# Top-k attention with two gated layers on one core: mask and exponential of the top-k moved from VectorE to two ScalarE passes

## The chip, the cores and the metric

One core of a Trainium2 chip runs the whole program. The metric is the device time of one execution in microseconds; the median of three runs is quoted. Engine names are those of the profile: PE is TensorE's matmul, PEld its weight load, DVE is VectorE, ACT is ScalarE, POOL is GpSimd, SP issues the DMAs.

## What is computed

The reference is an attention over the 32 largest scores of each row, a feed-forward layer with SiLU, and eight experts whose outputs are mixed by gates that are balanced in eight rounds. The change touches the attention alone:

```python
batch, n_heads, seq, head_dim = (2, 8, 576, 64)
scores = scale * np.matmul(q, k.transpose(0, 1, 3, 2))          # scale = 1 / 8
kth = np.partition(scores, -top_k, axis=-1)[..., -top_k:-top_k + 1]   # top_k = 32
mask = scores >= kth
scores = np.where(mask, scores, -1000000000.0)
scores = scores - np.max(scores, axis=-1, keepdims=True)
attn = np.exp(scores)
attn = attn / (np.sum(attn, axis=-1, keepdims=True) + 1e-09)
return np.matmul(attn, v).astype(np.float32)
```

The 1152 rows of attention output then go through x @ w_in, SiLU, @ w_out (512 to 2048 to 512), and each expert is relu(x @ w1[e]) @ w2[e] (512 to 1024 to 512), summed with its gate.

## The kernel before

The 1152 tokens are nine tiles of 128. Attention runs in five groups of queries, each over four pairs of heads. A unit is one group and one pair of heads; its score tiles are 128 queries by all 576 keys, 72 such tiles in all (64 of one head each, 8 half tiles that hold 64 queries of both heads of a pair). `score_tile` (L313) makes one of them:

- PE writes the scores into PSUM (L320), ACT copies them to an SBUF tile `s` (L323), of which the pool holds `SB` = 5.
- DVE finds the 32 largest by four rounds of eight: `max` (L332), and between rounds `match_replace` (L339), which overwrites the eight found in a work tile `w`.
- After the first round the largest value is known. A little row on POOL (on DVE in the first group, where `soon` is set) makes -scale * max (L335), and ACT takes the exponential of all 576 scores into a second tile `e` (L337), while DVE goes on searching.
- After the fourth round DVE compares the scores with the 32nd and multiplies by the exponentials in one instruction, which also gives the row's sum (L342).
- 1e-9 is added (L344, POOL or DVE), DVE takes the reciprocal (L345), ACT scales the row (L347), PE transposes it (L350, L352), ACT copies the transpose (L363, L364), and when a unit's tiles are done PE multiplies with V (L360, tile `pav`).

A scheduler orders the instructions of every engine ahead of time, by priorities that the kernel sets (`tc.cur_priority`), and each engine runs its list in order. Attention has the first claim; between its rows stand matmuls of the feed-forward layer and of experts as filler, in steps of a hidden block of weights: 12 matmuls of 128x256 (L145 to L149, `mm3`) into a PSUM bank, an activation on ACT and a split into two parts on ACT and POOL (L137, L138), then the second product (128x512 rows of L147 to L149), with weights that SP's queue loads. After the last unit of attention the rest of the filler runs, and from about 660 us on seven experts by a seven-product scheme.

The feed-forward weights come as 64-bit words in 32 blocks. Each is loaded into one of four buffers (`RAWB`, L529), converted by ACT (`narrow`, L493; the low word on POOL at L499 or on ACT at L497), and joined on DVE (L502). From block 12 on the joining rows are held until the last reciprocal of the first query group (`held`, L758, through `tc.issue_after`).

Of the kernel before, what the change touches and what calls it, by code (L numbers as in the profile page):

```python
# [8 lines left out]
F32 = mybir.dt.float32  # L9
# [3 lines left out]
AF = mybir.ActivationFunctionType  # L13
ALU = mybir.AluOpType
# [3 lines left out]
P = 128  # L18
TOPK = 32
# [19 lines left out]
WB = 4  # L39
RW = 6  # L40

SB = 5
SW = 2
AB = 2

# [27 lines left out]
def topk_attention_moe_sinkhorn_kernel(  # L73
# [12 lines left out]
    nc = tc.nc  # L86
    B, H, S, D = q.shape
# [6 lines left out]
    NTT = NT // P  # L94
    SH = S // 2
    SCALE = 1.0 / D ** 0.5
    MASKED = -1e9 / SCALE
    W = DM
    assert NDC * P == W

# [7 lines left out]
    const = ctx.enter_context(tc.tile_pool(name="const", bufs=1))  # L108
# [1 line left out]
    make_identity(nc, ident)  # L110
    ones = const.tile([P, P], F32, name="ones")
    nc.gpsimd.memset(ones, 1.0)
    neg = const.tile([P, 1], F32, name="neg")
    nc.gpsimd.memset(neg, MASKED)
    wg_raw = const.tile([P, NDC, NE], F32, name="wg_raw")
    wgH = const.tile([P, NDC, NE], F32R, name="wgH")
    wgL = const.tile([P, NDC, NE], F32R, name="wgL")
# [78 lines left out]
    sp = att.enter_context(tc.tile_pool(name="sp", bufs=SW))  # L196
# [116 lines left out]
    def score_tile(nm, qq, qL, kk, js, cols, soon, behind=None, late=False):  # L313

        ps = ps_s.tile([P, 2, 512], F32, name=f"ps_{nm}", tag="s")

        for j in js:
            for part, a in enumerate((qq, qL)):
                for hh in range(2):
                    nc.tensor.matmul(ps[:, hh, 0:SH], a[:, j, cols], kk[:, j, hh * SH : (hh + 1) * SH],  # L320
                                     start=j == js[0] and part == 0, stop=j == js[-1] and part == 1)
        s = sp.tile([P, S], F32, name=f"s_{nm}", tag="s", bufs=SB)
        copied.append(nc.scalar.activation(s.rearrange("p (a c) -> p a c", a=2), ps[:, :, 0:SH], AF.Copy))  # L323
        w = sp.tile([P, S], F32, name=f"w_{nm}", tag="w")
        m8 = small.tile([P, TOPK], F32, name=f"m8_{nm}", tag="m8")
        sm = small.tile([P, 4], F32, name=f"sm_{nm}", tag="sm")
        e = sp.tile([P, S], F32, name=f"e_{nm}", tag="e")
        src = s
        tiny = nc.vector if soon else nc.gpsimd
        for r in range(TOPK // 8):  # L330
            mr = m8[:, 8 * r : 8 * r + 8]
            nc.vector.max(mr, src)  # L332
            if r == 0:

                tiny.tensor_scalar(sm[:, 0:1], m8[:, 0:1], -SCALE, None, op0=ALU.mult)  # L335
                with tc.issue_after(behind.ins) if behind and late else nullcontext():
                    nc.scalar.activation(e, s, AF.Exp, scale=SCALE, bias=sm[:, 0:1])  # L337
            if r < TOPK // 8 - 1:
                nc.vector.match_replace(out=w, in_to_replace=mr, in_values=src, imm_value=-3e38)  # L339
                src = w  # L340

        nc.vector.scalar_tensor_tensor(s, s, m8[:, TOPK - 1 : TOPK], e, op0=ALU.is_ge, op1=ALU.mult,  # L342
                                       accum_out=sm[:, 1:2])
        tiny.tensor_scalar(sm[:, 2:3], sm[:, 1:2], 1e-9, None, op0=ALU.add)  # L344
        normal.append(nc.vector.reciprocal(sm[:, 3:4], sm[:, 2:3]))  # L345
        with tc.issue_after(behind.ins) if behind else nullcontext():
            nc.scalar.activation(s, s, AF.Copy, scale=sm[:, 3:4])  # L347
        pt = ps_t.tile([P, 4, P], F32, name=f"pt_{nm}", tag="tr")
        for c in range(4):
            nc.tensor.transpose(pt[:, c, :], s[:, c * P : (c + 1) * P], ident)  # L350
        pt2 = ps_t.tile([P, P], F32, name=f"pt2_{nm}", tag="tr")
        heads.append(nc.tensor.transpose(pt2, s[:, S - P : S], ident))  # L352
        return pt, pt2
# [793 lines left out]
```

## Time and profile before

| | |
|---|---|
| runs | 1222.16, 1222.31, 1222.91 us; median 1222.31 |
| profiled execution | 1223.83 us, of which the span from the first to the last instruction is 1222.0 |
| PE busy | 1176.0 us (96%), weight loads 949.6 |
| DVE, ACT, POOL busy | 800.5 (66%), 609.2 (50%), 593.2 (49%) |
| granted TensorE clock | 0.992 of full speed over the span |

Busy times are those of the profiler: a PE row is listed until its modelled end and overlaps the next, and rows of ACT and DVE overlap their neighbours by some hundredths to a tenth of a microsecond. The page also cuts the span into 40 slices of 30.6 us and gives each engine's busy share in tenths. DVE is at 9 from slice 2 to slice 16, with one exception at the first, and falls to 2 and 0 there: that is attention. PE is at 9 or more from slice 4 to the end.

```
PE   5797999999999999999999999999999999999998
DVE  7989999999999999203567634634445345344444
ACT  6856887788876877643313332332323223323212
```

### The profile page before, as it was taken

The numbers are of one execution on the slowest core, as the hardware profiler recorded it, in microseconds if no ns is written. First come the engines' busy times: TensorE is split into PE (matmuls) and PEld (weight loads), VectorE is DVE, ScalarE is ACT, GpSimd is POOL, SyncE is SP. The second block draws the span as 40 slices with busy tenths as digits, with TensorE's granted clock in tenths as the row PEclk, the third lists the DMA queues.
The fourth block names the chain that finished last, engine by engine and source line by source line (L and its number), as shares of the span: only waits on it lengthen the run. The fifth ranks groups of instructions, "written<-read, shape, count | busy, mean of one in ns | idle before, by whom it ended". The sixth has DMA issues, their size and how long they took to land.

```text
span 1222.0 us, 17930 instructions
## 1 busy us (share of the span) xinstructions
PE 1176.0 (96%) x6122; PEld 949.6 (78%) x6122; DVE 800.5 (66%) x1543; ACT 609.2 (50%) x1241; POOL 593.2 (49%) x665
## 2 busy tenths in 40 slices
PE   5797999999999999999999999999999999999998
PEld 3664666788778888888787888888888888888887
DVE  7989999999999999203567634634445345344444
ACT  6856887788876877643313332332323223323212
POOL 6666766788634843530546444445334444353310
PEclk9997999999999999999999999999999999999999
DMA  9889777998786898899814221121111211211001
GB/s 268 292 285 323 261 245 235 323 333 288 232 304 236 274 323 293 288 325 375 293 56 129 76 80 35 52 72 49 52 52 37 84 35 35 70 52 53 18 1 69
DMA packets 131723, 210.91 MB, mean 173 GB/s; under 512 B 23472, under 2 KB 69552, under 8 KB 131632
## 3 DMA queue, kind: packets, MB, share of 16 engines
q1 hardware_dynamic: 131632, 209.77, 51.4%
q8 instruction: 48, 0.79, 0.3%
q14 instruction: 43, 0.35, 0.1%
HBM read 170.15 MB, written 39.58 MB: 172 GB/s over the span
## 4 chain that ended last, share of the span: by engine, by line
PE 82%; DVE 11%; ACT 2%; DMA 1%; POOL 1%; issue 1%; SPq 0%; POOLq 0%; ACTq 0%; DVEq 0%
PE h L147 9%; PE h L148 9%; PE h L149 9%; PE bank L147 5%; PE bank L149 5%; PE bank L148 5%; PE yA L149 4%; PE yB L149 4%; PE yB L147 4%; PE yA L147 4%; PE yA L148 4%; PE yB L148 4%; PE bank L598 4%; DVE m L332 3%; PE pav L360 3%; DVE w L339 3%
## 5 line engine op out<-in xcount | busy, mean ns | idle before, releaser
L138 POOL TENSOR_TENSOR wp<-rw,wp 128x512 fp32r<-128x512 f32 (+1 forms) x56 | 86.7, 1567 | 195.2 <-ACT wp L137 195.2
L332 DVE MAX8 m<-w 128x8 f32<-128x576 f32 x192 | 140.0, 745 | 0.7
L138 POOL TENSOR_TENSOR wa<-raw,wa 128x512 fp32r<-128x512 f32 x88 | 114.9, 1318 | 29.6 <-ACT wa L137 14.2
L138 POOL TENSOR_TENSOR w<-rw,w 128x512 fp32r<-128x512 f32 x56 | 72.0, 1290 | 92.0 <-ACT w L137 92.0
L339 DVE MATCH_REPLACE8 w<-m,w 128x576 f32<-128x576 f32 x128 | 94.4, 739 | 0.0
L978 DVE SCALAR_TENSOR_TENSOR gL_0b<-gB,gH_0b 128x512 fp32r<-128x512 f32 (+1 forms) x56 | 44.5, 794 | 55.7 <-ACT gH_0b L977 54.8
L147 PE MATMUL yB<-w,gH_0b 128*128 128x512 f32 x208 | 80.9, 389 | 0.0
L148 PE MATMUL yB<-w,gH_0b 128*128 128x512 f32 x208 | 80.9, 389 | 0.0
L149 PE MATMUL yB<-w,gL_0b 128*128 128x512 f32 x208 | 80.1, 389 | 0.0
L977 ACT ACTIVATE gH_0b<-gB 128x512 fp32r<-128x512 f32 (+1 forms) x56 | 33.6, 600 | 76.1 <-PE yB L148 41.4
L148 PE MATMUL h<-x1L,wp 128*128 128x512 f32 x168 | 65.6, 391 | 0.0
L149 PE MATMUL h<-x1H,wp 128*128 128x512 f32 x168 | 65.6, 390 | 0.0
L147 PE MATMUL h<-x1H,wp 128*128 128x512 f32 x168 | 65.6, 390 | 0.0
L991 DVE TENSOR_TENSOR gB<-u,h 128x512 f32<-128x512 f32 x56 | 38.5, 687 | 35.6 <-PE h L149 35.5
L342 DVE SCALAR_TENSOR_TENSOR s<-s,m,e 128x576 f32<-128x576 f32 x64 | 61.2, 956 | 0.5
L137 ACT ACTIVATE w<-rw 128x512 fp32r<-128x512 f32 x56 | 34.6, 627 | 49.8 <-PE yB L149 48.3
L147 PE MATMUL bank<-xH,wa 128*128 128x256 f32 x192 | 57.2, 298 | 1.8 <-DVE g_m L449 1.1
L598 PE MATMUL bank<-wb,gT_e 128*128 128x512 f32 x128 | 58.2, 594 | 0.0
L347 ACT ACTIVATE s<-s,sm 128x576 f32<-128x576 f32 x64 | 49.9, 781 | 15.3 <-DVE sm L345 15.0
L137 ACT ACTIVATE wa<-raw 128x512 fp32r<-128x512 f32 x88 | 55.0, 648 | 3.2 <-DMA raw<-in_moe_w_dram 2.5
L138 DVE TENSOR_TENSOR wp<-sp,wp 128x1024 fp32r<-128x1024 f32 x28 | 45.3, 1617 | 15.3 <-ACT wp L137 15.3
L337 ACT ACTIVATE e<-s,sm 128x576 f32<-128x576 f32 x64 | 50.1, 784 | 8.4 <-DVE s L342 4.5
(376 smaller groups left out, 3670.6 us busy)
## 6 DMA issues: line engine op xcount, KB each, us to landing
wa<-sk SPq DMA_DIRECT2D x64, 512.0 KB, 5.5
wb<-sk SPq DMA_DIRECT2D x64, 512.0 KB, 5.3
rw<-in_moe_w_dram SPq DMA_DIRECT2D x112, 256.0 KB, 2.7
raw<-in_moe_w_dram SPq DMA_DIRECT2D x80, 256.0 KB, 3.8
wb<-in_moe_w_dram SPq DMA_DIRECT2D x32, 512.0 KB, 5.1
sk<-wa SPq DMA_DIRECT2D x24, 512.0 KB, 3.9
sk<-wb SPq DMA_DIRECT2D x24, 512.0 KB, 4.2
wfr<-in_moe_w_in_dram SPq DMA_DIRECT2D x16, 512.0 KB, 6.0
```

The costliest lines, as they stand in the source:

```text
L137: nc.scalar.activation(dH, src, AF.Copy)
L138: eng.tensor_sub(dL, src, dH.bitcast(F32))
L147: nc.tensor.matmul(ps, wH, xH, start=first, stop=False, skip_group_check=more)
L148: nc.tensor.matmul(ps, wH, xL, start=False, stop=False, skip_group_check=more)
L149: return nc.tensor.matmul(ps, wL, xH, start=False, stop=last, skip_group_check=more)
L332: nc.vector.max(mr, src)
L337: nc.scalar.activation(e, s, AF.Exp, scale=SCALE, bias=sm[:, 0:1])
L339: nc.vector.match_replace(out=w, in_to_replace=mr, in_values=src, imm_value=-3e38)
L342: nc.vector.scalar_tensor_tensor(s, s, m8[:, TOPK - 1 : TOPK], e, op0=ALU.is_ge, op1=ALU.mult, accum_out=sm[:, 1:2])
L347: nc.scalar.activation(s, s, AF.Copy, scale=sm[:, 3:4])
L598: nc.tensor.matmul(y, gT[:, c * P : (c + 1) * P], b[c], start=F == 0 and c == 0, stop=F == nF - 1 and c == NDC - 1)
L978: nc.vector.scalar_tensor_tensor(gL, src, 0.0, gH.bitcast(F32), op0=ALU.max, op1=ALU.subtract)
```

## The change

The exponential no longer runs beside the search. After the fourth round a little row makes scale * (32nd - max) from the 32nd value and the largest. ACT then takes two passes over `s` in place. The first is a parametric rectifier of 32nd - score: a score below the 32nd gives a positive difference, which is kept, and a score at or above it a difference of zero or less, which is multiplied by 2^-80. The second is an exponential with a scale of -scale * 2^80: it brings the kept scores' differences back to their size, and turns every other difference into an argument so far below zero that the result is zero. The second pass gives the row's sum. The compare-and-multiply on DVE, the tile `e` and its two buffers are gone; the tiles `s` go from 5 to 7. An unused constant goes as well.

```diff
-SB = 5
+SB = 7
-    MASKED = -1e9 / SCALE
+    BELOW = 2.0**-80
-    neg = const.tile([P, 1], F32, name="neg")
-    nc.gpsimd.memset(neg, MASKED)
...
-        e = sp.tile([P, S], F32, name=f"e_{nm}", tag="e")
         src = s
         tiny = nc.vector if soon else nc.gpsimd
         for r in range(TOPK // 8):
             mr = m8[:, 8 * r : 8 * r + 8]
             nc.vector.max(mr, src)
-            if r == 0:
-
-                tiny.tensor_scalar(sm[:, 0:1], m8[:, 0:1], -SCALE, None, op0=ALU.mult)
-                with tc.issue_after(behind.ins) if behind and late else nullcontext():
-                    nc.scalar.activation(e, s, AF.Exp, scale=SCALE, bias=sm[:, 0:1])
             if r < TOPK // 8 - 1:
                 nc.vector.match_replace(out=w, in_to_replace=mr, in_values=src, imm_value=-3e38)
                 src = w
-
-        nc.vector.scalar_tensor_tensor(s, s, m8[:, TOPK - 1 : TOPK], e, op0=ALU.is_ge, op1=ALU.mult,
-                                       accum_out=sm[:, 1:2])
+        kth = m8[:, TOPK - 1 : TOPK]
+        tiny.tensor_scalar(sm[:, 0:1], kth, m8[:, 0:1], SCALE, op0=ALU.subtract, op1=ALU.mult)
+
+        with tc.issue_after(behind.ins) if behind and late else nullcontext():
+            nc.scalar.activation(s, s, AF.Prelu, scale=-1.0, bias=kth, alpha=BELOW)
+            nc.scalar.activation(s, s, AF.Exp, scale=-SCALE / BELOW, bias=sm[:, 0:1], accum_out=sm[:, 1:2])
         tiny.tensor_scalar(sm[:, 2:3], sm[:, 1:2], 1e-9, None, op0=ALU.add)
```

The scheduler makes a new order of it. Two places follow. Names are tile<-tiles read, the last number of a name is the tile's instance and differs between the two programs; `wf_24` is weight block 24 in both, `s_0_0_3_1` the score tile of group 0, pair 3, second head. Lines after the change are two to five lower.

ACT at the end of the first query group, before: the exponentials of the last two tiles (`e_0_0_3_...`) stand ahead of block 24, the last of them in the first row here, and only their scaling by the reciprocal (L347, the last two rows) behind it.

```order
L337 ACTIVATE e_0_0_3_1_0_591<-s_0_0_3_1_0_586,sm_0_0_3_1_0_590 128x576
L347 ACTIVATE s_0_0_2_0_0_460<-s_0_0_2_0_0_460,sm_0_0_2_0_0_464 128x576
L493 ACTIVATE wf_23_639<-wfr_23_797 128x512
L347 ACTIVATE s_0_0_2_1_0_493<-s_0_0_2_1_0_493,sm_0_0_2_1_0_497 128x576
L493 ACTIVATE wf_24_638<-wfr_24_803 128x512
L363 ACTIVATE aT_0_0_2_0_453<-pt_0_0_2_0_0_479 128x4x128
L364 ACTIVATE aT_0_0_2_0_453<-pt2_0_0_2_0_0_484 128x128
L323 ACTIVATE s_1_0_0_0_1_1665<-ps_1_0_0_0_1_1660 128x576
L363 ACTIVATE aT_0_0_2_1_454<-pt_0_0_2_1_0_517 128x4x128
```

The same place now: L337 is the rectifier, L338 the exponential with the sum, L342 the scaling, L488 the conversion.

```order
L337 ACTIVATE s_0_0_3_0_0_545<-s_0_0_3_0_0_545,m8_0_0_3_0_0_548 128x576
L488 ACTIVATE wf_23_629<-wfr_23_787 128x512
L342 ACTIVATE s_0_0_2_1_0_486<-s_0_0_2_1_0_486,sm_0_0_2_1_0_490 128x576
L337 ACTIVATE s_0_0_3_1_0_577<-s_0_0_3_1_0_577,m8_0_0_3_1_0_580 128x576
L488 ACTIVATE wf_24_628<-wfr_24_793 128x512
L358 ACTIVATE aT_0_0_2_0_447<-pt_0_0_2_0_0_472 128x4x128
L338 ACTIVATE s_0_0_3_0_0_545,sm_0_0_3_0_0_549<-s_0_0_3_0_0_545,sm_0_0_3_0_0_549 128x576
L359 ACTIVATE aT_0_0_2_0_447<-pt2_0_0_2_0_0_477 128x128
L321 ACTIVATE s_1_0_0_1_1_1718<-ps_1_0_0_1_1_1713 128x576
L338 ACTIVATE s_0_0_3_1_0_577,sm_0_0_3_1_0_581<-s_0_0_3_1_0_577,sm_0_0_3_1_0_581 128x576
```

Both rectifiers now stand ahead of block 24, and both exponentials with the sum behind it.

PE just ahead of the last product with V (`pav_4_1_3`), before: the filler beside it belongs to the feed-forward layer of group 3, its weight tile `wa` number 412.

```order
L147 MATMUL bank2_134<-xH_3_5098,wa_412_5888 128x256
L148 MATMUL bank2_134<-xL_3_5099,wa_412_5888 128x256
L149 MATMUL bank2_134<-xH_3_5098,wa_412_5888 128x256
L360 MATMUL pav_4_1_3_6874<-aT_4_1_3_0_6740,vn_1_3_3732 64x256
L360 MATMUL pav_4_1_3_6874<-aT_4_1_3_1_6741,vn_1_3_3732 64x256
```

The same place now: the filler beside it is still the second product of an expert, `wb` number 393.

```order
L145 MATMUL bank1_131<-wb_393_4925,gH_e0_3_4_4940 128x512
L146 MATMUL bank1_131<-wb_393_4925,gH_e0_3_4_4940 128x512
L147 MATMUL bank0_130<-wb_393_4925,gL_e0_3_4_4941 128x512
L147 MATMUL bank1_131<-wb_393_4925,gL_e0_3_4_4941 128x512
L355 MATMUL pav_4_1_3_6800<-aT_4_1_3_0_6670,vn_1_3_3695 64x256
L355 MATMUL pav_4_1_3_6800<-aT_4_1_3_1_6671,vn_1_3_3695 64x256
```

Ahead of that product stand 46 matmuls of 512 columns and 92 of 256 fewer than before; all other rows there are as many. They follow after it.

## Rows read from the trace of the kernel before

**Rows 1.** The page, busy times, share of the span, number of instructions.
```profile
PE 1176.0 (96%) x6122; PEld 949.6 (78%) x6122; DVE 800.5 (66%) x1543; ACT 609.2 (50%) x1241; POOL 593.2 (49%) x665
```

**Rows 2.** Chain of waits, three PE pieces: start us, us on the chain, what.
```profile
215.06 0.23 PE bank L147
...
249.28 0.12 PE bank L147
...
504.90 1.88 PE pav L360 x16
```

**Rows 3.** Windows: stretch, length, busy us of each engine, clock, DMA share, GB/s.
```profile
core 0: us, PE busy (x) PEld busy (x) DVE busy (x) ACT busy (x) POOL busy (x), PEclk, DMA share, GB/s
120.00:500.00 380.00, 374.91 (x2341) 293.00 (x2340) 370.38 (x826) 302.00 (x664) 234.01 (x316) 1.00 0.82 279
500.00:660.00 160.00, 155.73 (x876) 130.56 (x875) 61.49 (x132) 60.62 (x139) 65.88 (x67) 0.99 0.71 248
660.00:1222.00 562.00, 558.03 (x2463) 461.75 (x2461) 261.96 (x353) 164.35 (x281) 218.48 (x203) 1.00 0.18 53
```

**Rows 4.** Groups by line, whole run: busy us, mean ns | idle before.
```profile
L342 DVE SCALAR_TENSOR_TENSOR s<-s,m,e 128x576 f32<-128x576 f32 x64 | 61.2, 956 | 0.5
L342 DVE DVE_READ_ACCUMULATOR s<-s,m,e 128x1 f32 x64 | 5.0, 78 | 0.0
L337 ACT ACTIVATE e<-s,sm 128x576 f32<-128x576 f32 x64 | 50.1, 784 | 8.4 <-DVE s L342 4.5 <-POOL sm L335 3.6
L447 ACT ACTIVATE t_m<-bank 128x256 f32<-128x256 f32 x48 | 18.6, 388 | 26.1 <-PE bank L149 25.7
L452 ACT ACTIVATE t_m<-t_m 128x256 f32<-128x256 f32 x32 | 13.7, 428 | 0.0
L364 ACT ACTIVATE aT<-pt_h 128x64 f32<-128x64 f32 x16 | 2.9, 248 | 0.0
```

**Rows 5.** Windows of one line alone: L342 on DVE twice, L337 on ACT.
```profile
0.00:68.00 68.00, 7.33 (x16) 0.97 0.91 291
...
120.00:500.00 380.00, 61.20 (x120) 1.00 0.82 279
...
120.00:500.00 380.00, 45.61 (x58) 1.00 0.82 279
```

**Rows 6.** Timeline of ACT near the first group's end: start us, us, instruction [idle before].
```profile
59.04 0.67 ACT L493 ACTIVATE wf<-wfr 128x512 f32<-128x512 f32 x1 [0.57 <-DMA wfr<-in_moe_w_out_dram]
59.62 0.76 ACT L337 ACTIVATE e<-s,sm 128x576 f32<-128x576 f32 x1
60.29 0.76 ACT L347 ACTIVATE s<-s,sm 128x576 f32<-128x576 f32 x1
...
63.55 0.67 ACT L493 ACTIVATE wf<-wfr 128x512 f32<-128x512 f32 x1 [1.16 <-DMA wfr<-in_moe_w_out_dram]
64.12 0.57 ACT L363 ACTIVATE aT<-pt 128x512 f32<-128x512 f32 x1
64.60 0.26 ACT L364 ACTIVATE aT<-pt 128x128 f32<-128x128 f32 x1
64.76 0.65 ACT L323 ACTIVATE s<-ps 128x576 f32<-128x576 f32 x1
```

**Rows 7.** Windows of 40 us, columns as in rows 3.
```profile
400.00:440.00 40.00, 37.34 (x251) 31.94 (x250) 39.20 (x87) 35.60 (x82) 32.01 (x42) 1.00 0.86 292
...
560.00:600.00 40.00, 39.28 (x249) 33.17 (x247) 14.79 (x29) 13.82 (x31) 10.03 (x10) 1.00 0.94 347
```

**Rows 8.** Waits in 120 to 500 us: who for whom, us, times, longest.
```profile
ACT t_m L447 <- PE bank L149: 13.2, 15, 2.9
...
ACT e L337 <- POOL sm L335: 3.6, 5, 1.7
...
POOL sm L344 <- DVE s L342: 24.5, 12, 4.7
```

**Rows 9.** Chain of waits, end of the first group.
```profile
67.83 3.61 DVE wf L502 x6
```

**Rows 10.** Timeline of ACT, first instruction.
```profile
0.71 1.28 ACT L250 ACT_TABLE_LOAD   x1 [0.71 <-PEq L1131]
```

## The prediction

> **What bounds the kernel now.** I read the page first, then the windows by stage, then the chain of waits, and only then single lines. The page [rows 1] shows TensorE (PE) busy 96% of the span, which is not the bound it seems: the listed ends of matmuls are modelled and overlap, while on the chain of waits a 512-column one counts 0.23 us and a 256-column one 0.12 [rows 2], so a busy PE may still stand still between two rows. The windows [rows 3] tell the stages apart. From 120 to 500 us (attention of query groups 1 to 4, with feed-forward filler in between) VectorE (DVE) is the engine that is never free: 370.4 of 380 us, 97.5%, where ScalarE (ACT) has 302.0, 79%. The first query group ends on DVE as well: the chain of waits goes from its last rows there into the conversion of the weights [rows 9]. From 500 us on DVE has little to do, and after 660 us PE has 558.0 of 562: that last part can't be touched by this change. Attention is therefore the only place to win, and DVE the engine that sets its pace.
>
> **The change, part by part.**
>
> *DVE.* The compare-and-multiply goes, 72 times (64 and 8 of the half tiles; the 64 average 956 ns [rows 4]), with its accumulator read. By stage it is 61.2 us in 120 to 500 and 7.33 us in the first group [rows 5]. DVE in 120 to 500 falls to 370.4 - 61.2 = 309 us, 81% of the old length: it stops being the bound.
>
> *ACT.* One exponential becomes a rectifier and an exponential with a sum: one more pass over 128x576 for each of the 58 tiles of that stretch [rows 5]. A pass is listed with 0.78 us [rows 4], but its successor starts 0.67 us after it (59.62 to 60.29 [rows 6]); I take 58 x 0.67 = 38.9 us. The read of ACT's accumulator is nowhere in this trace. Its bounds are zero and the smallest copy of ACT, 0.25 us (128x64 [rows 4]); I take 0.1, of the order of DVE's own read, 78 ns [rows 4]: 58 x 0.1 = 5.8 us.
>
> *Order.* The scheduler puts attention earlier. Counted in the two orders, 46 matmuls of 512 columns and 92 of 256 fewer stand ahead of the last probability-times-V product on PE: 46 x 0.23 + 92 x 0.12 = 21.6 us of PE work that must be done later, at the pace of 500 to 660 us (155.7 of 160 us busy [rows 3]), so 22.2 us. Twelve of the 256-column ones make a step, so 7.7 steps move, with their ACT work (a tanh of 0.39 us and up to three copies of 0.43 [rows 4], 12.9 us in all) and their loads, two of 512 KB a step on SP's queue, 8.1 MB: at the 347 GB/s of 560 to 600 us [rows 7] that is 23.2 us beside PE's 22.2, so SP's queue is no worse a limit than PE by more than 1 us.
>
> *ACT's new sum* in the stretch: 302.0 + 38.9 + 5.8 - 12.9 = 333.8 us. It becomes the fullest engine, and the stretch lasts 333.8 us divided by the share that it can be kept busy. Below is the fullest 40 us that ACT has now, 35.6 of 40, 89%, with DVE at 98% beside it [rows 7]; above is what DVE reached as the bound, 97.5%. I take 95%, nearer the upper one, because ACT now mostly waits for PE (13.2 us for the tanh alone [rows 8]): it has caught up with its supplier, and an engine with a backlog does not wait so. 333.8 / 0.95 = 351.4 us, 28.6 less than 380.
>
> *The first group.* DVE loses 7.33 us of work here, and I count almost nothing of it. The conversion of the feed-forward weights waits for the last reciprocal of this group and starts at 67.83 us [rows 9]. In the new order the last two exponentials stand on ACT behind the conversion of weight block 24, and that row waits for its DMA: now it starts at 63.55 us after 1.16 us of idling for the transfer [rows 6]. Behind it, by the spacings in [rows 6]: its own 0.57, a copy 0.48, exponential 0.77, small copy 0.16, copy 0.65, exponential 0.77, then about 0.35 for addition and reciprocal on DVE: 67.3 us. Gain 0.5 us. If block 24 came as much earlier as DVE is faster, the gain would be 7.33 less the two ACT passes of the last tile (about 1.5) and their handing over, some 5 us; that is the other bound. The block follows a ring of four buffers, not the top-k, so I stay at 0.5.
>
> *Small edits at nothing.* The negated maximum becomes a subtract-and-multiply of the same 128x1 size on the same engine. The two buffers of the exponential go and the scores get seven instead of five: a tile now keeps its scores through two more ACT passes, some 2 us, with a new tile every 380 / 58 = 6.6 us, and the two added buffers cover it; without them ACT's copy of the next scores would wait.
>
> *Sum.* -28.6 + 22.2 - 0.5 = -6.9 us, against the profiled execution's 1223.83 us, which lies 1.5 us above the median of the runs (1222.31): 1216.9 there, **1215.4 us** as a median.
>
> *A rule against the change.* The 64 compare-and-multiplies average 956 ns on DVE, and an ACT pass of the same 128x576 averages 784 [rows 4]: by the rows, work of 61.2 us leaves DVE and 44.7 comes to ACT. The Trainium skill, in "ScalarE: Activation LUTs" under the rules for kernel authors, says that rectifiers, maxima and products belong on VectorE, which it puts at up to about three times faster per element in bf16. By that rule ACT would be given what DVE does in a third of its pass, 58 x 0.26 = 15 us, and the trade would be 15 off for 44.7 on; these float32 rows show no such lead of DVE.
>
> **The rivals.**
>
> *A, the forecast.* ACT is kept busy 94 to 97.5% of the stretch, which then lasts 355.1 to 342.4 us: 1219 to 1206 us.
>
> *B, the first group gains too.* Weight block 24 comes earlier with everything else, and some 5 us come off instead of 0.5: 1211 us. For it: transfers of the later blocks wait for buffers that conversions free. Against it: the DMA wait in [rows 6] at a moment when DVE was the late one.
>
> *C, a draw.* At 93.2% the stretch is 358.3 us, 21.7 shorter, and the matmuls that were moved behind it take all of that back: 1222 us. What shrinks is then only the wait, and it reappears as filler. For it: ACT and PE hand single PSUM buffers to each other, so neither can run far ahead.
>
> *D, slower: ACT's queue stops at the exponential.* In the old order the exponential needed the maximum of the first round and had the whole search to hide POOL's little subtraction. Now the subtraction starts after the 32nd value is known, on POOL's queue behind splits, and the exponential waits for it in ACT's queue, with evacuations of PE's banks behind it. ACT has waited 3.6 us, 5 times, for such a POOL row already, and POOL 24.5 us for DVE's sum [rows 8], which becomes a wait for ACT. If each of the 58 exponentials costs ACT 0.25 us of waiting, 14.5 us, the stretch is 365.9, and the sum -14.1 + 22.2 - 0.5: 7.6 us slower, 1230 us. Above 0.16 us a tile (9.3 us) it decides for slower. The orders put several rows between rectifier and exponential, which speaks against it.
>
> *E, the function tables.* If the rectifier needed another table than the exponential, each tile would load two. The one load of this trace took 1.28 us [rows 10], so 144 loads are 184 us: 1406 us. Against it: rectifier and exponential already follow each other at 59.04 and 59.62 us with no load in between [rows 6], and both orders hold a single load. The Trainium skill says the same price in "ScalarE: Activation LUTs", What ACT_TABLE_LOAD costs: about 1.28 us and a drain of about 1.38 for a switch to a different set, which would make it 383 us here; the trace agrees on the first and has no switch to show the second.
>
> **How the numbers follow.** A measurement of this kernel tells a change from none at about 0.2%, 2.4 us. Faster by more needs ACT above 93.8%, slower by more below 92.5%. I give A 0.47 (0.02 of it within 2.4 us), B 0.10, C 0.15, D 0.27, E 0.01. So faster 0.45 + 0.10 = 0.55; same 0.02 + 0.15 = 0.17; slower 0.28. With ACT at 97.5% and a free accumulator read the stretch is 328.0 / 0.975 = 336.4, the time 1200; with 89% and a read of 0.25 us it is 342.5 / 0.89 = 384.8, the time 1249. Of these ends I leave 1 in 10 on either side: 1203 to 1232; the forecast's own range is 1206 to 1219.
>
> **What would show it.** Right: in 120 us to the end of attention DVE's share falls to about 88% and ACT's rises to 95%; the last probability-times-V product, now at 504.9 us [rows 2], comes near 476; rows of PE after it are the filler that was moved, 22 us longer; the weight conversion still starts at about 67 us. Wrong: ACT below 92% with idle time before the exponential put down to POOL (D), or the conversion starting at 62 us (B); a second table load (E). The whole falls if the stretch is not shorter at all, that is, if DVE never set its pace, or if PE stalls behind 500 us where the moved work goes.

## The result, and the profile after

The changed kernel took 1239.24 us (median of 4 runs, 1238.70 to 1240.08) where the kernel before took 1222.24 beside it: 1.0139 times as long, 95% interval 1.0122 to 1.0157. It is slower by 17 us; the forecast was 1215.4, range 1203 to 1232. The profiled execution took 1239.21 us with a span of 1237.4, 15.4 more than before.

First the busy times of the page, as in [rows 1]: DVE did lose 58 us and ACT gained 46, and PE is as full as it was.

```profile
PE 1186.5 (96%) x6122; PEld 950.0 (77%) x6122; DVE 742.9 (60%) x1399; ACT 655.4 (53%) x1385; POOL 578.3 (47%) x664
```

The windows by stage, columns as in [rows 3]:

```profile
120.00:500.00 380.00, 372.93 (x2276) 284.12 (x2276) 321.51 (x703) 338.09 (x775) 220.65 (x314) 1.00 0.79 265
500.00:660.00 160.00, 157.03 (x896) 133.08 (x895) 54.21 (x115) 60.49 (x144) 65.06 (x71) 0.99 0.74 274
660.00:1237.00 577.00, 573.11 (x2507) 469.90 (x2505) 266.63 (x367) 168.34 (x288) 225.04 (x207) 1.00 0.18 54
```

In the attention stretch ACT is now fuller than DVE, as forecast. But PE has 2276 rows there instead of 2341: it does *less* of its work in the same 380 us. What PE gets done there turns out to matter, not DVE's share. The engine shares of the chain of waits point the same way; before:

```profile
PE 82%; DVE 11%; ACT 2%; DMA 1%; POOL 1%; issue 1%; SPq 0%; POOLq 0%; ACTq 0%; DVEq 0%
```

and after:

```profile
PE 88%; DVE 5%; ACT 3%; DMA 3%; issue 1%; POOL 0%; SPq 0%; ACTq 0%; POOLq 0%
```

These shares take in the expert phase, where PE is nearly alone. In 120 to 500 us by itself the chain ran over PE for 76% and over DVE for 15% before, and runs over them for 89% and 6% now: over PE for the most part even when DVE was listed at 97.5%. Only in the first 120 us was DVE the larger part (61% before).

**An account by PE.** Both kernels give PE the same 6122 matmuls. I valued each kind (source line and shape) at the spacing that it usually has in the kernel before (the 30th percentile of start to next start: 227 ns for most rows of 512 columns, 119 for 256, 132 for 288, 108 to 112 for most transposes). The sum is 1119.7 us for either kernel. What is left of a stage's length is PE's stall (waits, and rows that ran at the lower of TensorE's two clocks, 1.2 instead of 2.4 GHz). Stages are bounded by the first probability-times-V row of the 5th unit (group 1's first), the last such row, and the first ACT copy of expert 0.

| stage | before: length = rows + stall | after | difference |
|---|---|---|---|
| to the 5th unit | 127.2 = 67.4 + 59.8 | 133.6 = 72.3 + 61.3 | +6.4 |
| 5th to last unit | 381.0 = 352.7 + 28.2 | 363.0 = 326.3 + 36.6 | -18.0 |
| to expert 0 | 138.4 = 129.0 + 9.4 | 160.6 = 150.5 + 10.1 | +22.2 |
| experts, end | 575.4 = 570.6 + 4.9 | 580.2 = 570.6 + 9.7 | +4.8 |
| sum | 1222.0 = 1119.7 + 102.4 | 1237.4 = 1119.7 + 117.7 | +15.4 |

So the attention stretch is 18 us shorter because 26.4 us of PE's rows left it (4.9 went ahead of it, 21.5 behind), and it is worse inside by 8.4 us of stalls. The rest is 4.8 us in the expert phase, where the change touches nothing, 1.5 in the first part and 0.7 in the third.

**Where PE waits.** The longest wait in the stretch is at 330 us. ACT's timeline there (start us, us, instruction):

```profile
328.24 0.68 ACT L358 ACTIVATE aT<-pt 128x512 f32<-128x512 f32 x1
328.72 1.76 ACT L135 ACTIVATE wa<-raw 128x512 fp32r<-128x512 f32 x3
330.28 0.86 ACT L337 ACTIVATE s<-s,m 128x576 f32<-128x576 f32 x1
330.94 0.85 ACT L342 ACTIVATE s<-s,sm 128x576 f32<-128x576 f32 x1
331.61 0.36 ACT L359 ACTIVATE aT<-pt 128x128 f32<-128x128 f32 x1
331.76 0.86 ACT L338 ACTIVATE s<-s,sm 128x576 f32<-128x576 f32 x1
332.43 0.29 ACT L338 ACTIVATION_READ_ACCUMULATOR s<-s,sm 128x1 f32 x1
332.52 0.73 ACT L321 ACTIVATE s<-ps 128x576 f32<-128x576 f32 x1
```

and PE's, those rows that waited:

```profile
332.02 0.33 PE L347 MATMUL pt<-ident,s 128*128 128x128 f32 x1 [2.14 <-ACT aT L359]
333.31 0.85 PE L318 MATMUL ps<-kk,qq 128*128 128x288 f32 x2 [0.96 <-ACT s L321]
```

ACT has no idle time here. The copy that empties the transpose bank (L359) stands behind three weight splits, a rectifier and a scaling, and PE's next transpose waits 2.14 us for it; the score matmuls wait another 0.96 for L321, behind an exponential. At these two waits the granted clock fell; the window, columns as in [rows 3]:

```profile
330.00:340.00 10.00, 7.02 (x20) 4.12 (x21) 9.69 (x22) 8.92 (x19) 4.25 (x7) 0.83 0.47 148
```

A clock of 0.83 over 10 us is 3.4 us at the lower level, 1.2 GHz, which adds up to 1.7 us to the stall; in the kernel before the whole stretch ran at 2.4 GHz [rows 3]. So a wait of PE can cost more than its own length. This one place is shown; how the rest of the 8.4 us is spread was not worked out row by row.

ACT's own waits, 120 to 500 us:

```profile
ACT t_m L442 <- PE bank L147: 8.2, 10, 1.3
...
ACT s L338 <- POOL sm L334: 0.6, 1, 0.6
```

and POOL's:

```profile
POOL sm L339 <- ACT s L338: 40.1, 26, 3.3
```

ACT waited once, 0.6 us, for POOL's subtraction; POOL's small addition waits for ACT where it waited 24.5 us for DVE [rows 8].

### The profile page after: what moved, and what is told of

Its sections match the earlier page's. It is cut to its first block, busy times and chain, and to the rows that moved or that the text cites. A ratio compares the mean times of both kernels' runs of the same rounds, so it can differ in the third digit from the quotient of the medians.

```text
span 1237.4 us, 17954 instructions
## 1 busy us (share of the span) xinstructions
PE 1186.5 (96%) x6122; PEld 950.0 (77%) x6122; DVE 742.9 (60%) x1399; ACT 655.4 (53%) x1385; POOL 578.3 (47%) x664
## 4 chain that ended last, share of the span: by engine, by line
PE 88%; DVE 5%; ACT 3%; DMA 3%; issue 1%; POOL 0%; SPq 0%; ACTq 0%; POOLq 0%
PE h L145 9%; PE h L147 9%; PE h L146 8%; PE bank L145 6%; PE bank L147 6%; PE bank L146 6%; PE bank L593 5%; PE yA L145 4%; PE yA L146 4%; PE yA L147 4%; PE yB L145 4%; PE yB L147 4%; PE yB L146 4%; PE pav L355 4%; DVE m L329 2%; PE ps L318 2%
## 5 line engine op out<-in xcount | busy, mean ns | idle before, releaser
L136 POOL TENSOR_TENSOR wa<-raw,wa 128x512 fp32r<-128x512 f32 x88 | 112.2, 1287 | 26.7 <-ACT wa L135 21.2
L136 POOL TENSOR_TENSOR w<-rw,w 128x512 fp32r<-128x512 f32 x56 | 72.3, 1296 | 91.0 <-ACT w L135 91.0
L355 PE MATMUL pav<-aT,vn 128*64 128x256 f32 (+3 forms) x480 | 55.6, 348 | 2.2 <-ACT aT L358 2.2
L329 DVE MAX8 m<-s 128x8 f32<-128x576 f32 x64 | 47.7, 749 | 11.9 <-ACT s L321 11.7
L342 ACT ACTIVATE s<-s,sm 128x576 f32<-128x576 f32 x64 | 52.8, 830 | 3.6 <-DVE sm L340 3.6
```

The costliest lines, as they stand in the source:

```text
L136: eng.tensor_sub(dL, src, dH.bitcast(F32))
L355: nc.tensor.matmul(ps[r, :n], vn[:, j, c, :], aT[j][:, c, :n], start=c == 0, stop=c == 4)
```

## The experiments

All times are medians beside runs of the kernel before on the same chip (1221 to 1222.5 us). "Stall" is PE's in the profiled execution, by the account above, from the 5th to the last unit unless another stage is named.

### The place of the tiles: e1, e2, f1

The change deletes `neg`, a constant that nothing read. Its 4 bytes took 32, so every tile on the left side of the memory slid down by 32 bytes; many had started at multiples of 64.

**e1_keep_const**: the change, with the constant kept.

```
     nc.gpsimd.memset(ones, 1.0)
+    neg = const.tile([P, 1], F32, name="neg")
+    nc.gpsimd.memset(neg, -1e9 / SCALE)
```

> The changed kernel with the unused 4-byte constant left in place, so that every left-side tile lies 32 bytes higher, where it lay in the kernel before; all engines but POOL (one memset more) have the same rows in the same order. Theory (place of the tiles slows PE and ACT rows by up to 4%): the stretch behind expert 0's first copy takes 575 to 576 us again instead of 580.2, an ACT scaling pass is back near 781 ns from 830, and the time is 1231 to 1234 us. Rival (the slower rows come from the new order, or from the clock): 580 us there, scaling pass at 820 to 830 ns, and 1238 to 1240 us.

Measured: 1235.94 us, ratio 1.0114 (1.0090 to 1.0137), between the ranges of theory and rival; expert phase 574.6 us, as the theory has it. The other half failed: the scaling pass is listed at 838 ns in the stretch, as in the changed kernel. So ACT's longer listing is not a matter of place. A full queue alone does not make it either: in e6 below, with ACT busy 86%, the scaling pass is listed at 785. What does is not shown.

**e2_shift_only**: the kernel before without that constant.

```
-    neg = const.tile([P, 1], F32, name="neg")
-    nc.gpsimd.memset(neg, MASKED)
```

> The kernel before without its unused 4-byte constant, and nothing else changed: left-side tiles lie 32 bytes lower, the orders are the same. Theory (place of the tiles): the expert phase is 4 to 5 us longer and the time is 1227 to 1232 us. Rival (the place is indifferent): 1222 us, within 1.5.

Measured: 1228.99 us, ratio 1.0055 (1.0036 to 1.0075), the theory, with not one row moved on any engine but POOL, which loses the memset. The expert phase is 581.0 us; the stretch is unchanged (stall 28.3). The medians put the constant's price at 7.0 us here and at 3.3 between the changed kernel and e1, the expert phase of the profiled executions at 5.6 both times. PE's timeline in the expert phase, kernel before:

```profile
900.99 0.39 PE L147 MATMUL h<-x1H,wp 128*128 128x512 f32 x1
901.21 0.39 PE L148 MATMUL h<-x1L,wp 128*128 128x512 f32 x1
901.44 0.39 PE L149 MATMUL h<-x1H,wp 128*128 128x512 f32 x1
```

and e2:

```profile
900.15 0.40 PE L145 MATMUL h<-x1H,wp 128*128 128x512 f32 x1
900.39 0.39 PE L146 MATMUL h<-x1L,wp 128*128 128x512 f32 x1
900.62 0.40 PE L147 MATMUL h<-x1H,wp 128*128 128x512 f32 x1
```

The starts stand 0.22 to 0.23 us apart before and 0.23 to 0.24 in e2. Over the phase h<-x1H,wp has a mean spacing of 232.2 ns against 226.7, h<-t1H,wp 235.2 against 226.7, and yB<-w,gH stays at 226.7.

**f1_pad_back**: e2 with the pad ahead of the expert weights 32 bytes larger.

```
-    pad("pad_l", 64, reuse_waits="tile")
+    pad("pad_l", 96, reuse_waits="tile")
```

> The kernel of e2_shift_only with the pad ahead of the expert weights 32 bytes larger: the weights wp and all that is allocated behind them lie where they lay in the kernel before, x1, its sums t2 to t4 and the accumulators still 32 bytes lower. Theory (what slows the matmuls h<-x1,wp and h<-t,wp is the place of the moving x1 and t tiles): still 1226 to 1230 us, spacing of h<-x1H,wp 232 ns. Rival (the place of the weights does): 1221 to 1223 us, 227 ns.

Measured: 1229.63 us, ratio 1.0060 (1.0038 to 1.0082), so moving the weights back does not help; but the slow rows are not the same. h<-x1H,wp is at 229.0 ns, h<-t3H,wp and h<-t4H,wp at 233.6 and 233.8 (228.6 and 227.5 in e2). The place of x1 and of the sums t2 to t4 matters too, then. For x1 the addresses in the programs tell more. Each of its two parts lies in two pieces. The larger piece of the high part (tile `x1H`) moved in none of these kernels: its rows stand at 226.7 ns before, at 234.9 in e2, where the weights alone had moved, and at 226.8 in f1, where neither had. The smaller piece (`x1H_4`) moved both times: 226.7 in e2, where the weights had moved with it by the same 32 bytes, and 233.3 in f1, where it had moved alone. So for x1 it is the place relative to the weights, not either place by itself. The sums follow this only in part (t3 and t4 stand at 228.6 and 227.5 in e2, though they moved with the weights; t1, which never moved, at 229.5 in f1), and that stays open.

### DVE's load and ACT's, one at a time: e4, e5, e6, e11

**e5_dve_relief**: the kernel before without the compare-and-multiply.

```
-                    nc.scalar.activation(e, s, AF.Exp, scale=SCALE, bias=sm[:, 0:1])
+                    nc.scalar.activation(e, s, AF.Exp, scale=SCALE, bias=sm[:, 0:1], accum_out=sm[:, 1:2])
...
-        nc.vector.scalar_tensor_tensor(s, s, m8[:, TOPK - 1 : TOPK], e, op0=ALU.is_ge, op1=ALU.mult,
-                                       accum_out=sm[:, 1:2])
-        tiny.tensor_scalar(sm[:, 2:3], sm[:, 1:2], 1e-9, None, op0=ALU.add)
+        tiny.tensor_scalar(sm[:, 2:3], m8[:, TOPK - 1 : TOPK], sm[:, 1:2], 1.0, op0=ALU.add, op1=ALU.mult)
...
-            nc.scalar.activation(s, s, AF.Copy, scale=sm[:, 3:4])
+            nc.scalar.activation(s, e, AF.Copy, scale=sm[:, 3:4])
```

> The kernel before without the compare-and-multiply: the exponential (still early, under the search) is taken of all scores and sums itself, and its result is scaled and transposed; the mask is left out. The small addition before the reciprocal takes the 32nd value as well, so the reciprocal still waits for the search, and its result is not the sum. DVE loses 64 full and 8 half rows, ACT gets no pass. Theory of the forecast (DVE sets the pace of the attention stretch): 1202 to 1214 us. Rival (PE's own rows set it: 6122 matmuls whose pace at full clock adds up to 1119.7 us in both kernels, plus PE's stalls, of which the stretch from the 5th to the last probability-times-V unit has only 28 us; so DVE's relief can give back a part of these): 1216 to 1222 us.

Measured: 1216.87 us, ratio 0.9961 (0.9944 to 0.9978), the rival; stall 26.6 us. Its window:

```profile
120.00:500.00 380.00, 378.24 (x2346) 293.30 (x2345) 314.46 (x688) 306.54 (x720) 221.48 (x315) 1.00 0.82 275
```

DVE fell from 370 to 314 us with ACT at 307 where it had 302, and the kernel gained 5 us. The premise of the forecast fails here: DVE was full, but did not set the time. Its stretch is 20.8 us shorter than before, yet 19.2 of that are rows of PE that moved out of it. The freest version of the idea, with no mask at all and no pass added, won 5 us in the one order that it was given.

**e6_act_load**: the kernel before with an idle copy on ACT per tile.

```
                     nc.scalar.activation(e, s, AF.Exp, scale=SCALE, bias=sm[:, 0:1])
+                    nc.scalar.activation(e, e, AF.Copy)
```

> The kernel before with one more ACT pass per tile, a copy of the exponential onto itself right behind it; DVE's rows are unchanged and every result as before. Theory of the forecast (DVE at 97.5% sets the pace and ACT with 302 + 39 of 380 us still has room): 1222 to 1226 us. Rival (PE waits for ACT's evacuations, and a fuller ACT serves them later, whatever DVE does): 1230 us or more, stalls of PE in the stretch above 36 us.

Measured: 1237.80 us, ratio 1.0130 (1.0114 to 1.0147); stall 36.9 us: the rival. The window:

```profile
120.00:500.00 380.00, 369.07 (x2277) 285.21 (x2276) 368.64 (x810) 325.50 (x704) 228.58 (x309) 1.00 0.81 272
```

ACT is busy 86% and DVE 97%, and yet PE is behind by 64 rows: nearly the same shortfall as in the changed kernel.

**e4_no_rectifier**: e1 without the rectifier pass, so that no score is masked.

```
-            nc.scalar.activation(s, s, AF.Prelu, scale=-1.0, bias=kth, alpha=BELOW)
-            nc.scalar.activation(s, s, AF.Exp, scale=-SCALE / BELOW, bias=sm[:, 0:1], accum_out=sm[:, 1:2])
+            nc.scalar.activation(s, s, AF.Exp, scale=SCALE, bias=sm[:, 0:1], accum_out=sm[:, 1:2])
```

> The kernel of e1_keep_const without the rectifier pass: the exponential is taken of every score, so nothing is masked; its sum is still taken. 64 full and 8 half passes fewer on ACT, DVE's rows as in the changed kernel. Theory of the forecast (ACT's sum sets the length of the attention stretch, filler moved behind it gives most back): last probability-times-V product at 475 us or before, against 493 in the changed kernel, and the time 4 to 10 us under e1_keep_const. Rival (PE sets the time: its own rows and its stalls; ACT's extra pass is only one of many waits): the stretch is shorter by under 10 us and the time within 3 us of e1_keep_const.

Measured: 1222.05 us, ratio 0.9996 (0.9983 to 1.0008), 14 under e1 and more than either theory gave; stall 30.0. The forecast's picture of it fails in the same run: the last unit starts at 489.2 us, not 475, so it is not a shorter stretch that pays.

**e11_scale_on_dve**: e1 with the scaling on DVE.

```
-            nc.scalar.activation(s, s, AF.Copy, scale=sm[:, 3:4])
+            nc.vector.tensor_scalar(s, s, sm[:, 3:4], None, op0=ALU.mult)
```

> The kernel of e1_keep_const with the scaling by the reciprocal on DVE in place of ACT: ACT gives back one pass per tile (45 us in the stretch) and DVE, which the change relieved of 61, gets one row of 128x576 per tile. Theory (PE waits for a full ACT): ACT's work is that of the kernel before plus 6 us, so 1219 to 1226 us, 10 to 16 under e1_keep_const. Rival (the longer chain of one tile, or the order, makes the loss): 1231 us or more.

Measured: 1224.73 us, ratio 1.0023 (1.0013 to 1.0033), 11 under e1, the theory; stall 30.8. The new DVE row, as a group over the whole run:

```profile
L344 DVE TENSOR_SCALAR s<-s,sm 128x576 f32<-128x576 f32 x64 | 44.6, 699 | 0.1
```

The rule of the Trainium skill against this change ("ScalarE: Activation LUTs", rules for kernel authors: products belong on VectorE) has the sign right here. The row's mean hides two kinds: 35 of the 64 take 494 to 520 ns (median of all 509, against 777 for ACT's scaling before), the other 29 on average 935 and up to 1460. The long ones have a POOL row running beside them for 88% of their time, the short ones for 30%. So most rows are a third shorter on DVE, not two thirds. What else came with the gain is that ACT has a pass per tile fewer.

### Half of the tiles: e7, g1

```
+        fresh = not soon and int(nm.split("_")[3]) % 2 == 1 if not nm.endswith("h") else False
...
+        if fresh:
+            tiny.tensor_scalar(sm[:, 0:1], kth, m8[:, 0:1], SCALE, op0=ALU.subtract, op1=ALU.mult)
+            with tc.issue_after(behind.ins) if behind and late else nullcontext():
+                nc.scalar.activation(s, s, AF.Prelu, scale=-1.0, bias=kth, alpha=BELOW)
+                nc.scalar.activation(s, s, AF.Exp, scale=-SCALE / BELOW, bias=sm[:, 0:1], accum_out=sm[:, 1:2])
+        else:
+            nc.vector.scalar_tensor_tensor(s, s, kth, e, op0=ALU.is_ge, op1=ALU.mult, accum_out=sm[:, 1:2])
```

(g1 has `== 0` for `== 1`; the fourth part of a tile's name is the head.)

> The kernel before with only the full tiles of the second head of each pair, in groups 1 to 4, by the rectifier and the exponential with its sum; all others by the old path, constant kept, five score buffers. DVE -25 us and ACT +20 us in the stretch. Rival (ACT's fullness is what PE waits for, growing with each extra pass): between the two kernels, 1226 to 1232 us. Theory of the forecast (balance of DVE and ACT counts: 345 and 322 us): 1214 to 1220 us.

> The kernel of e7_half_tiles with the first head of each pair by the new path instead of the second, everything else the same. Theory (e7's stalls were those of its order; half of the passes cost half): PE's stalls from the 5th to the last unit 31 to 36 us, time 1226 to 1233 us. Rival (two paths of unequal length side by side make PE, whose order is fixed, wait): 38 us of stalls or more, 1235 us or more.

Measured: e7 1238.92 us, ratio 1.0137 (1.0122 to 1.0152), stall 41.0; g1 1224.64 us, ratio 1.0016 (1.0006 to 1.0025), stall 30.4. Neither expectation for e7 held, and g1 came out better than its theory. The two kernels have the same amounts of work and stand 14 us apart; only which head goes which way differs, and with it the order that the scheduler wrote. Up to half of the difference in stall is the clock: in e7 the granted clock is 0.83 in 320 to 340 us and 0.91 in 420 to 440, which is 10 us at the lower level, 1.2 GHz, and up to 5 us lost, each time at a wait of PE for ACT (2.87 and 2.02 us). In g1 it is 1.00 all through the stretch.

### How much is the order: e3, e8, e9, e10, e12, f2, f3, f4, g2

**e3_copy_first.** In the changed kernel PE stood idle before 80 us; ACT's timeline there:

```profile
76.92 0.66 ACT L488 ACTIVATE wf<-wfr 128x512 f32<-128x512 f32 x1 [3.26 <-DMA wfr<-in_moe_w_out_dram]
78.20 0.66 ACT L488 ACTIVATE wf<-wfr 128x512 f32<-128x512 f32 x1 [0.62 <-DMA wfr<-in_moe_w_out_dram]
78.77 0.65 ACT L492 ACTIVATE cv_n<-wfr 128x512 int32<-128x512 uint32 x1
79.49 0.68 ACT L488 ACTIVATE wf<-wfr 128x512 f32<-128x512 f32 x1
80.08 0.25 ACT L403 ACTIVATE x<-pav 128x128 f32<-128x128 f32 x1
```

and PE's row that waited:

```profile
80.39 2.94 PE L544 MATMUL bank<-x,wf 128*128 128x128 f32 x13 [4.29 <-ACT x L403]
```

The copy of the first group's last result stands behind conversions that wait for their DMA. The edit (`x0_copies` collects these copies) orders it ahead of them:

```
-        nc.scalar.activation(x, hi.bitcast(F32), AF.Prelu, scale=2.0**-112, alpha=-(2.0**32))
+        with tc.issue_after(x0_copies[-1].ins) if i >= 25 else nullcontext():
+            nc.scalar.activation(x, hi.bitcast(F32), AF.Prelu, scale=2.0**-112, alpha=-(2.0**32))
```

> The kernel of e1_keep_const with the last copy of the first group's attention result put on ACT ahead of the conversion of weight blocks 25 and later, which wait for their DMA. Theory (this copy behind DMA-paced conversions makes the first part 5 to 6 us longer): the first x1 transpose, 101.0 us in the changed kernel and 96.1 before, comes at 95 to 97, and the time is 4 to 6 us under that of e1_keep_const. Rival (the DMA-paced conversions themselves, or the lower clock after PE's idling, set the time whichever row stands first): the transpose stays at 100 or later and the time within 1.5 us of e1_keep_const.

Measured: 1234.91 us, ratio 1.0101 (1.0079 to 1.0123). The copy came at 78.24, behind one conversion still, and the x1 transpose at 100.1: the rival. The first part's stall fell by 2.5 us and the stretch's rose by 5.2 (41.8) in the order that resulted.

**e8_silu_on_dve**: e3, with the gate function's DVE form in all steps.

```
-            if late or nm.startswith("m1"):
+            if True:
```

> The kernel of e3_copy_first with the second half of the gate function of all feed-forward steps as one DVE row from PSUM (as group 1 has it already), in place of two ACT copies and a POOL product: ACT loses about 16 us in the stretch, DVE gets about 9. Theory (ACT's fullness is what PE waits for): 5 to 12 us under e3_copy_first, so 1223 to 1230 us. Rival (what costs is the longer chain of one tile: search, rectifier, exponential in sequence, however full ACT is): within 3 us of e3_copy_first.

Measured: 1233.57 us, ratio 1.0094 (1.0079 to 1.0110), stall 39.1: within 3 us of e3, the rival. But it tests less than it was meant to: ACT's listed time in 120 to 500 us fell by 6.6 us only (335.9 in e3, 329.3 here), not by 16, where e4 and e11 took 31 and 32 off (338.0 in e1, 307.1 and 306.0). PE's largest waits here, in sum over 120 to 500 us, are for the end of a tile's chain: 3.8 us for ACT's scaling pass and 3.4 for the copy ahead of the product with V. So a longer chain of one tile is not ruled out as a part of the loss. Against it as the whole stand e6, which fills ACT beside the search and stalls 36.9 us, and e11, which keeps the chain and stalls 30.8.

**e9_other_order** and **f4_changed_order**: the kernel before and e1, each with `LATE = 11` for 12.

> The kernel before with the same work in another order: the 12th weight block's join, not only the 13th and later, waits for the last reciprocal of the first group, and some 330 of 5117 rows of PE's order stand elsewhere. Theory (it is the added ACT work that costs): 1220 to 1225 us. Rival (any order but the one chosen for exactly this work puts rows where PE waits for them, and the change's loss is one of order): 1228 us or more, stalls of PE from the 5th to the last probability-times-V unit above 33 us (28 in the kernel before).

> The kernel of e1_keep_const (the whole change, constant kept) with the same work in another order: the 12th weight block's join, not only the 13th and later, waits for the first group's last reciprocal. Theory (ACT's added pass is the larger part of the loss, order the smaller): 1230 to 1240 us, like all versions with the full added pass so far. Rival (order is the larger part): at or under 1227 us.

Measured: e9 1229.82 us, ratio 1.0062 (1.0045 to 1.0079), stall 31.9, and 3.1 us more than before in the first part: the time of the rival, but a stall under its bound of 33. f4 1235.32 us, ratio 1.0109 (1.0093 to 1.0125), stall 37.6: the theory.

**e10_five_buffers**: e1 with `SB = 5` for 7.

> The kernel of e1_keep_const with five score buffers instead of seven. The forecast gave the two added buffers out as cover that is needed: without them ACT's copy of the next scores waits, 3 to 8 us slower than e1_keep_const, 1239 to 1244 us. Rival (a tile's longer hold of its buffer is well under five tiles' time): within 3 us of e1_keep_const, 1233 to 1239.

Measured: 1231.28 us, ratio 1.0075 (1.0058 to 1.0091): 4.7 faster than e1 where the forecast's reason wanted it slower. That is under the rival's range as well. Two more buffers were no needed cover, and they came with another order.

**e12_scale_and_hop**, **f2_dve_scale_five**, **f3_five_no_hop**: e11 with e3's edit and the reciprocal taken straight from the sum (below); e11 with `SB = 5`; f2 with the reciprocal likewise.

```
-        tiny.tensor_scalar(sm[:, 2:3], sm[:, 1:2], 1e-9, None, op0=ALU.add)
-        normal.append(nc.vector.reciprocal(sm[:, 3:4], sm[:, 2:3]))
+        normal.append(nc.vector.reciprocal(sm[:, 3:4], sm[:, 1:2]))
```

> The kernel of e11_scale_on_dve with the first group's last copy ahead of the conversions (as in e3_copy_first) and without the addition of 1e-9 to the sum: the sum is at least 1, so the addition changes no bit, and the reciprocal takes ACT's sum without a turn over POOL or DVE. Theory (shorter first part, one handing over fewer per tile): 1 to 5 us under e11_scale_on_dve, 1215 to 1222 us, level with the kernel before or a little under. Rival (handing over is hidden): within 1.5 us of e11_scale_on_dve.

> The kernel of e11_scale_on_dve with five score buffers. Theory (five are enough, and the order that they give was 4.7 us better in e10): 1216 to 1222 us. Rival (the gain of e10 was that of one order and is not carried over): 1223 to 1230 us.

> The kernel of f2_dve_scale_five without the addition of 1e-9, the reciprocal taking ACT's sum directly. Theory (one handing over fewer per tile shortens the chain that PE's transposes wait for): 1 to 4 us under f2. Rival (orders differ by more than this saves): anywhere within 5 us of f2, above as well as below.

Measured: e12 1227.39 us, ratio 1.0044 (1.0030 to 1.0057); f2 1232.42, 1.0083 (1.0061 to 1.0105); f3 1233.54, 1.0090 (1.0064 to 1.0116). For e12 neither expectation held, f2 came out 2 us beyond its rival's range, and f3 as its rival says. In the stretch e12 and f3 are good (stalls 28.2 and 29.3), f2 less so (31.6). All three lose in the first part (e12 63.2, f2 64.2, f3 69.8, against 57.5 in e11). The profiled execution of e12 is the fastest of its ten, 1224.76 us, so its stalls show 2.6 us less than its median lost.

**g2_before_no_hop**: the kernel before with the same edit, which only takes work away.

> The kernel before without the addition of 1e-9 to the sum (the sum is at least 1, so no bit changes); the reciprocal on DVE takes the sum that DVE has just made, without a turn over POOL. Theory (DVE's 5.4 us of waiting for POOL and the chain of every tile are shorter): 1216 to 1221 us. Rival (PE's order and stalls decide, and a new order costs what it costs): 1222 to 1232 us.

Measured: 1235.86 us, ratio 1.0111 (1.0096 to 1.0126), slower than even the rival gave, with 38.0 us of stall in the stretch and 63.5 in the first part. Its window:

```profile
120.00:500.00 380.00, 370.01 (x2261) 282.97 (x2260) 373.72 (x812) 290.11 (x638) 214.92 (x250) 1.00 0.80 270
```

A needless small row removed, ACT listed with 290.1 us, and 13 us lost against the kernel before.

### Taken together

| ACT passes added | kernels (all with the constant) | stall, 5th to last unit | us |
|---|---|---|---|
| on all tiles | e1, e3, e6, e8, e10, f4 | 34.9 to 41.8, mean 37.8 | 1231.3 to 1237.8 |
| on half | e7, g1 | 41.0, 30.4 | 1238.9, 1224.6 |
| none or given back | before, e4, e5, e9, e11, e12, f2, f3, g2 | 26.6 to 38.0, mean 30.5 | 1216.9 to 1235.9 |

The kernels with the added pass on all tiles stall 7 us more on average, and the two sets overlap only in g2. In time they lose 10.1 to 16.0 us to the kernel before, 13.0 on average; the eight others of the last row stand 4.9 under to 13.3 over it, 6.1 over on average. By these averages about half of the 14 us that e1 loses goes with the pass, and about half with giving up the order of the kernel before. But kernels of like work differ by as much (e9, f2, f3 and g2 lose 9 to 13 us with no ACT pass added on balance), so no single pair of runs proves a few microseconds here. By ACT's listed time in 120 to 500 us it reads alike: at 325 us or more the stall is 34.9 to 41.8, under 320 it is 26.6 to 31.9, but for e7 (311 us, 41.0) and g2. No kernel that does the reference's computation was faster than the kernel before; e4 and e5 leave out the mask.

The place of the tiles shows in all of them: in the seventeen kernels with the constant the expert phase has 3.7 to 5.4 us of stall, in the three without it (the changed kernel, e2, f1) 9.7, 10.5 and 10.0.

## Why the prediction was wrong, point by point

- **What bounds the kernel: wrong, and this is the step that failed.** "Attention is therefore the only place to win, and DVE the engine that sets its pace" was read from busy shares. e5 took 56 us off DVE and gained 5; e6 left DVE at 97%, put a pass on ACT and lost 16. PE set the time: its rows are worth 1119.7 us wherever they stand, and only its stalls can be won, 28.2 us in the stretch. The text warned itself with its last sentence, "if DVE never set its pace". Of the 22.3 us between the forecast sum (-6.9) and the profiled difference (+15.4), 10.6 stand in the stretch, 6.9 in the first part and 4.8 in the expert phase.
- **The stretch: -28.6 forecast, -18.0 measured.** The terms of ACT's sum were right: a pass starts 0.66 to 0.67 us before its successor, the accumulator's read 0.09 to 0.10 (below), and ACT had 338.1 us in the window against 333.8. The share was not: 95% forecast, 328.6 of 360 us or 91% in 120 to 480. By that share the sum would have been 365.6 us, 14.4 shorter, and the time about 7 us over the kernel before; but to divide ACT's work by a share was the wrong sum. The stretch shrank since 26.4 us of PE's rows were ordered out of it, while stalls grew by 8.4.
- **The moved filler: +22.2 forecast, +22.2 measured** for the third stage. The order told the 21.6 us of rows (21.5 measured). That the sums agree to a tenth is luck: the forecast's other 0.6 was a pace, the measured 0.7 is stall. Missed: 4.9 us of PE's rows moved *ahead* of the stretch as well, which is most of the first part's +6.4.
- **The first group: -0.5 forecast.** The conversion began at 66.75 us (67.83 before, 67.3 forecast): near. The 7.33 us taken off DVE gained nothing more: in the first 120 us its share of the chain of waits fell from 61% to 26%, and PE (24%), DMA (20%) and ACT (18%) took its place. The part as a whole grew by 1.5 us of stall besides the moved rows; the sum had no term for PE's waits behind the conversion, such as the 4.29 us for the copy at 80.08 (lines at e3).
- **Small edits at nothing: wrong by 4.8 us.** The prediction did not speak of the deleted constant. e1 and e2 show its price from both sides with every order kept; it is the one item of the loss that is isolated. The buffers' cover was not needed (e10).
- **Rivals.** D had the sign and was 9 us short, for a wrong reason: the exponential waited 0.6 us for POOL in all, not 14.5. Its other half, "evacuations of PE's banks behind it", is what happened, behind passes, not behind a wait. B and E did not occur. C, "What shrinks is then only the wait, and it reappears as filler", came nearest to the account by PE.

The accumulator's read, ACT's timeline at the end of the first group:

```profile
64.13 0.77 ACT L338 ACTIVATE s<-s,sm 128x576 f32<-128x576 f32 x1
64.80 0.19 ACT L338 ACTIVATION_READ_ACCUMULATOR s<-s,sm 128x1 f32 x1
64.89 0.27 ACT L359 ACTIVATE aT<-pt 128x128 f32<-128x128 f32 x1
```

Listed with 0.19 us, it holds up its successor by 0.09.

What stays open: which rows of an order cost the 9 to 13 us that e9, f2, f3 and g2 lose without added ACT work on balance. The order was never held fixed while the work changed; a schedule is written anew for every edit, so the added pass and its order were not separated further than the table does.

## What to carry to other kernels

Where PE has the same rows in both versions, add them up at their usual spacing by stage first: the rest is stall, and no relief of another engine can win more than that, however full the engine is listed. When a scheduler writes the order, an edit is worth its work plus a new order; make a few versions of equal work before believing a difference of 1%. And compare the addresses of tiles when an unused one is deleted.

## What was not expected of the hardware

A shift of 32 bytes of PE's operands, with no row moved, slowed 512-column matmuls from 226.7 to as much as 235.2 ns in the mean and cost 5.6 us of span (e2) in the expert phase, while the same shift left the attention stretch as it was (stall 28.2 and 28.3). Putting the weights back alone moved the slowness to other rows without lessening it (f1, 10.0 us of stall in that phase against 10.5). For x1 the rows are slow where its place has shifted by 32 bytes relative to the weights (234.9 and 233.3 ns) and at the old speed where both or neither have shifted (226.7 and 226.8); the sums follow this only in part.
